# Attention scores contracted over 64 partitions a head, with unpadded keys, in a fused attention and MLP kernel on one Trainium2 core

The kernel runs on one core of one Trainium2 chip. The metric is the device time of one execution, in microseconds (us). The kernel before takes 275.12 us (median of 2 runs, 274.87 to 275.37).

## The reference

Causal attention over 4 batches, 8 heads, 768 positions and head size 64, then an MLP. Heads 0, 2 and 6 ("retrieval") see all earlier positions; the other five ("streaming") see 4 sink positions and a window of 64.

```python
scores = scale * np.matmul(q, k.transpose(0, 1, 3, 2))      # q, k: (4, 8, 768, 64), scaled by 0.1
mask   = np.where(retr, causal, causal & (is_sink | in_win))
a      = softmax(np.where(mask, scores, -1e9))
x      = np.matmul(a, v).transpose(0, 2, 1, 3).reshape(3072, 512)
h      = x @ w_in                                           # (512, 2048)
out    = np.maximum(0.01 * h, h) @ w_out                    # (2048, 512)
```

## The kernel before

The kernel works on 8 chunks of 384 positions (two a batch). The engines run in a fixed order; the attention of chunk n+1 is woven between the MLP matmuls of chunks n and n-1.

For each pair of heads, TensorE transposes keys and queries (both heads at once: 2 x 64 = 128 partitions). The queries are copied out in one piece. The keys are copied in two, each head into a tile of its own whose other 64 partitions are zero:

```python
kt = [bf(f"kt{i}", 4, 2, S) for i in range(2)]         # pair, half, position
def zeros(i):
    nc.vector.memset(kt[i][64:128, :, 0, :], 0.0)
    nc.vector.memset(kt[i][0:64, :, 1, :], 0.0)
    ...
# prep_pair
for hh in range(2):
    r = slice(64 * hh, 64 * hh + 64)
    move(eng[hh], kt[i][r, p, hh, CH * c : CH * c + CH], pt[r, 0, 0:3, :])
move(eng[2], qts[n][:, p, :], pt[:, 1, 0:3, :])
```

A score matmul then contracts over all 128 partitions, and the zeros remove the other head's queries. The work is cut into *units*: one group of keys of a retrieval head (one or two matmuls), or a whole streaming head (six matmuls of 64 columns). The `qk` part of a unit (scores, exp, mask) is issued, and two slots later its `do_av` part.

```python
nc.tensor.matmul(s[:, off : off + w], lhsT=kt[i][:, p, hh, 128 * kj : 128 * kj + 128],
                 rhs=qts[n][:, p, lo:CH], ...)
```

The softmax here doesn't subtract the row's maximum and nothing guards it: scores larger than these inputs give would overflow.

Of the kernel before, what the change touches and what calls it, by code (L numbers as in the profile page):

```python
# [17 lines left out]
CH = 384  # L18
# [3 lines left out]
def kernel(  # L22
# [12 lines left out]
    nc = tc.nc  # L35
    B, H, S, D = q.shape
    assert (B, H, S, D) == (4, 8, 768, 64)
    NS = int(n_sink)
# [17 lines left out]
    def bank(tag, shape, dtype):  # L56
        return ps.tile(shape, dtype, name=tag, tag=tag, bufs=BANKS[tag])
# [44 lines left out]
    def bf(name, *shape):  # L102
        return one.tile([128, *shape], BF16, name=name)
# [5 lines left out]
    e_sink = bf("e_sink", 128)  # L109
    m_sink = bf("m_sink", H, D + 1)  # L110
    shift = bf("shift", 2, 128)
    kt = [bf(f"kt{i}", 4, 2, S) for i in range(2)]
    va = [bf(f"va{i}", 6, H, D + 1) for i in range(2)]
    vb = [bf(f"vb{i}", 5, H, D + 1) for i in range(2)]
    vs = [bf(f"vs{i}", H, D + 1) for i in range(2)]
    ksink = [bf(f"ksink{i}", 4, 128) for i in range(2)]
# [6 lines left out]
                                channel_multiplier=cm, pattern=pattern)  # L123

    def zeros(i):
        eng = nc.vector
        eng.memset(kt[i][64:128, :, 0, :], 0.0)
        eng.memset(kt[i][0:64, :, 1, :], 0.0)
        nc.gpsimd.memset(va[i][:, :, :, D], 1.0)
        nc.gpsimd.memset(ksink[i][:], 0.0)  # L130
        nc.gpsimd.memset(vs[i][:, 0, :], 0.0)

    def constants():
        make_identity(nc, ident)
        zeros(0)
        nc.gpsimd.memset(m_caus[:], 1.0)
        keep(m_caus[:], [[1, 128]], ALU.is_ge, 0, -1)
        nc.gpsimd.memset(m_win[:], 1.0)
        keep(m_win[:], [[0, 6], [-1, 64]], ALU.is_gt, 0, 1)
        keep(m_win[:], [[0, 6], [1, 64]], ALU.is_ge, 64, -1)  # L140

        nc.gpsimd.memset(shift[:], 0.0)
        nc.gpsimd.memset(e_sink[:], 0.0)
# [23 lines left out]
    qts = {}  # L167

    def qk_src(nm, n):
        pat = "p (g h d) -> p g h d" if n >= WIDE else "p (h g d) -> p g h d"  # L170
        return stage[nm, n].rearrange(pat, h=H, g=3)

    def v_src(n):
        return stage["v", n].rearrange("p (g h d) -> p g h d", g=3, h=H)
# [42 lines left out]
    def prep_pair(n, p, tag="pt", eng=("v", "v", "v")):  # L217
        b, c = divmod(n, 2)
        i = b % 2
        if p == 0:  # L220
            qts[n] = rot.tile([128, 4, CH], BF16, name="qt", tag="qt", bufs=2)
        pt = bank(tag, [128, 2, 4, 128], BF16)
        for e, nm in enumerate("kq"):
            for g in range(3):
                nc.tensor.transpose(pt[:, e, g, :], cast[nm, n][:, g, 2 * p : 2 * p + 2, :], ident[:])  # L225

        def move(e, dst, src):
            if n < WIDE:

                src = src.rearrange("p g t -> p t g")  # L230
                dst = dst.rearrange("p (t g) -> p t g", g=3)
            else:
                dst = dst.rearrange("p (g t) -> p g t", g=3)
            if e == "v":
                nc.vector.tensor_copy(dst, src)  # L235
            else:
                nc.scalar.activation(out=dst, in_=src, func=ACTF.Copy)

        for hh in range(2):
            r = slice(64 * hh, 64 * hh + 64)  # L240
            move(eng[hh], kt[i][r, p, hh, CH * c : CH * c + CH], pt[r, 0, 0:3, :])
        move(eng[2], qts[n][:, p, :], pt[:, 1, 0:3, :])


# [3 lines left out]
    class Attention:  # L248
# [32 lines left out]
        def sink(self, values=True):  # L281
            i, c = self.i, self.c
            if c == 0:
                for h in range(H):
                    if not IS_RETR[h]:
                        p, hh = h // 2, h % 2
                        r = slice(64 * hh, 64 * hh + 64)
                        nc.vector.tensor_copy(ksink[i][r, p, NS * h : NS * h + NS], kt[i][r, p, hh, 0:NS])
                if values:
                    self.sink_values()  # L290
            s = self.score()
            w = CH - self.sink_lo
            for p in range(4):
                nc.tensor.matmul(s[:, 0:w], lhsT=ksink[i][:, p, :], rhs=qts[self.n][:, p, self.sink_lo : CH],
                                 start=(p == 0), stop=(p == 3))
            self.at_sink = rot.tile([128, CH], BF16, name="at_sink", tag="at_sink", bufs=2)
            nc.scalar.activation(out=self.at_sink[:, self.sink_lo : CH], in_=s[:, 0:w], func=ACTF.Exp, scale=SM)

        def retr(self, h):
            p, hh = divmod(h, 2)  # L300
            i, c, n = self.i, self.c, self.n
            groups = [[(0, 0)], [(1, 128), (2, 256)]] if c == 0 else \
                [[(kj, 0)] for kj in range(4)] + [[(4, 128), (5, 256)]]
            r = []
            for grp in groups:
                box = {}

                def qk(grp=grp, box=box):
                    s = self.score()
                    a = rot.tile([128, CH], BF16, name="at", tag="at", bufs=6)  # L310
                    off = 0
                    for j, (kj, lo) in enumerate(grp):
                        w = CH - lo
                        nc.tensor.matmul(  # L314
                            s[:, off : off + w], lhsT=kt[i][:, p, hh, 128 * kj : 128 * kj + 128],
                            rhs=qts[n][:, p, lo:CH], start=(j == 0), stop=(j == len(grp) - 1),
                            skip_group_check=True)
                        off += w
                    nc.scalar.activation(out=a[:, 0:off], in_=s[:, 0:off], func=ACTF.Exp, scale=SM)  # L319
                    off = 0  # L320
                    for (kj, lo) in grp:
                        if kj >= 3 * c:
                            nc.vector.tensor_mul(a[:, off : off + 128], a[:, off : off + 128], m_caus[:])  # L323
                        off += CH - lo
                    box[0] = a

                def do_av(grp=grp, box=box):
                    off = 0
                    for (kj, lo) in grp:
                        for qi in range(lo // 128, 3):  # L330
                            o = off + 128 * qi - lo
                            self.av(p, hh, qi, box[0][:, o : o + 128], va[i][:, kj, h, :])
                        off += CH - lo

                r.append((qk, do_av, p))
            return r

        def stream(self, h):
            p, hh = divmod(h, 2)
            i, c, n = self.i, self.c, self.n  # L340
            box = {}

            def qk():
                s = self.score()
                a = ats[ats_i[0] % len(ats)]
                ats_i[0] += 1
                for m in range(6):
                    k0 = 64 * max(6 * c + m - 1, 0)
                    nc.tensor.matmul(  # L349
                        s[:, 64 * m : 64 * m + 64], lhsT=kt[i][:, p, hh, k0 : k0 + 128],  # L350
                        rhs=qts[n][:, p, 64 * m : 64 * m + 64], start=(m == 0), stop=(m == 5),
                        skip_group_check=True)
                av_ = a[:, :, 0:4:3, :]
                nc.scalar.activation(  # L354
                    out=av_, in_=s[:, 0:CH].rearrange("p (j e f) -> p j e f", j=3, e=2),
                    func=ACTF.Exp, scale=SM)
                m_ = (m_win0 if c == 0 else m_win).rearrange("p (j e) f -> p j e f", j=3)
                nc.vector.tensor_mul(av_, av_, m_)  # L358
                box[0] = a

            def do_av():
                a = box[0]
                for j in range(3):
                    t = 3 * c + j
                    ve = va[i][:, 0, h, :] if t == 0 else vb[i][:, t - 1, h, :]
                    self.av(p, hh, j, a[:, j, 0:2, :], ve)
                    self.av(p, hh, j, a[:, j, 2:4, :], va[i][:, t, h, :])

            return [(qk, do_av, p)]
# [107 lines left out]
    def preps(n):  # L477
        return [lambda p=p: prep_pair(n, p) for p in range(4)]
# [4 lines left out]
    lo, hi = slice(0, 4), slice(4, 8)  # L483
    k0, q0, v0 = qk_src("k", 0), qk_src("q", 0), v_src(0)
# [12 lines left out]
    nc.gpsimd.tensor_copy(ktb[:, :, hi], k0[:, :, hi])  # L497
    late_constants()
    prep_pair(0, 0, "pt", "vva")
    prep_pair(0, 1, "py", "aav")  # L500
    qk(*R0)
# [49 lines left out]
    a1 = Attention(1, po_tags=("po", "po", "po", "py")).slots(order=[0, 2, 6, 1, 3, 4, 5, 7])  # L551
    run(a1[0:6], merge(in_slots(0), a1[6:]))
    zeros(1)
    cast_qk(2)
    load(3, "k", eng=nc.gpsimd)
# [62 lines left out]
```

## Time and profile before

| | before |
|---|---|
| time, median | 275.12 us |
| span of the profile | 273.6 us |
| TensorE (PE) busy | 240.9 us, 88% |
| VectorE (DVE) / ScalarE (ACT) busy | 119.5 / 142.0 us |
| mean granted clock of TensorE | 0.994 |
| start of the MLP of chunk 2 / of chunk 7 | 94.8 / 239.1 us |

The last row cuts the run into three: a start in which PE waits now and then, a full stretch of 144.3 us in which it doesn't (attention of chunks 3 to 7 among the MLP matmuls), and the end, in which there is only the MLP. I call the middle one the full stretch; its ends are the first `w_in` matmuls of MLP chunks 2 and 7. The busy time of PE is a sum of durations that overlap, so the starts of matmuls are what to read.

In the lines of the profile, PSUM tiles have these names: `psS` scores, `po` attention times values, `pt` transposes, `ph` and `py` the two matmuls of the MLP (weights `w_in` and `w_out`). `kt` and `qt` are the transposed keys and queries, `at` and `ats` the exponentiated scores, `va` and `vb` the values and their copy shifted by 64 positions, `xs` the attention output.

### The profile page before, as it was taken

The page shows a single profiled execution, that of the slowest core. Times are in us where ns is not written, and L with a number is a line of the kernel's source. Part 1 is how long each engine was busy: PE and PEld are TensorE (multiplying, and loading weights), DVE is VectorE, ACT ScalarE, POOL GpSimd, SP SyncE. Part 2 cuts the span into 40 slices and gives each one's busy share as a digit, 9 for nine tenths or more (in the row PEclk, how much of TensorE's full clock was granted, in tenths as well). Part 3 has the DMA queues.
Part 4 walks back from the last instruction along what each step waited for, and adds up shares of the span by engine and source line. Part 5 has one row for each costly group of instructions (what it writes and reads, how often), then busy time and mean ns, then how long its engine had stood idle before and what let it go on. Part 6 is the DMA issues. An engine that isn't in the chain of part 4 may idle for free.

```text
span 273.6 us, 5398 instructions
## 1 busy us (share of the span) xinstructions
PE 240.9 (88%) x2164; PEld 148.4 (54%) x2164; DVE 119.5 (44%) x323; ACT 142.0 (52%) x309; POOL 70.8 (26%) x122
## 2 busy tenths in 40 slices
PE   1647498857897899999999999999999999999995
PEld 1426365635553456665666556665665566545544
DVE  5669315766633514544545335544463224311012
ACT  3545787726740076555464666555555676633300
POOL 5889279764520034000420043000000000000000
PEclk9999889999999999999999999999999999999999
DMA  7999999999931298109940795120111111001122
GB/s 214 269 214 185 249 218 206 231 226 200 212 86 40 80 226 156 39 2 185 201 118 4 151 198 136 38 78 2 41 40 56 45 38 41 4 37 38 38 79 77
DMA packets 58281, 32.11 MB, mean 117 GB/s; under 512 B 44816, under 2 KB 53264, under 8 KB 58256
## 3 DMA queue, kind: packets, MB, share of 16 engines
q1 hardware_dynamic: 51792, 21.12, 33.2%
q0 software_dynamic: 5664, 8.91, 17.3%
q10 hardware_dynamic: 800, 1.73, 2.9%
q8 instruction: 17, 0.28, 0.4%
q14 instruction: 8, 0.07, 0.1%
HBM read 27.26 MB, written 6.29 MB: 123 GB/s over the span
## 4 chain that ended last, share of the span: by engine, by line
PE 75%; DVE 13%; ACT 7%; issue 2%; DMA 2%; SPq 0%; ACTq 0%; DVEq 0%
PE py L444 27%; PE ph L431 25%; PE po L266 6%; PE psS L314 4%; PE pt L225 3%; PE psS L444 3%; DVE kt L235 3%; DVE ats L358 2%; DVE at L323 2%; DVE xs L378 2%; ACT at L319 2%; PE pt L384 2%; PE psS L349 2%; DMA f<-in_q_dram 2%; ACT ats L354 1%
## 5 line engine op out<-in xcount | busy, mean ns | idle before, releaser
L431 PE MATMUL ph<-xt,w_in_bf 128*128 128x384 bf16 x512 | 104.7, 327 | 0.0
L433 ACT ACTIVATE g<-ph 128x384 bf16<-128x384 f32 x128 | 62.9, 491 | 76.1 <-PE ph L431 75.1
L444 PE MATMUL py<-w_out_bf,g 128*128 128x512 bf16 (+1 forms) x352 | 91.2, 374 | 3.2 <-DVE o L449 2.9
L431 PEld LDWEIGHTS <-w_in_bf 128*128 128x128 bf16 x512 | 44.9, 98 | 24.7 <-issue 0.3
L444 PEld LDWEIGHTS <-g 128*128 128x128 bf16 x400 | 36.0, 97 | 31.2 <-issue 5.4
L319 ACT ACTIVATE at<-psS 128x384 bf16<-128x384 f32 x81 | 39.2, 489 | 13.2 <-PE psS L314 12.7
L323 DVE TENSOR_TENSOR at<-at,m_caus 128x128 bf16<-128x128 bf16 x72 | 20.1, 310 | 47.2 <-ACT at L319 46.9
L314 PE MATMUL psS<-qt,kt 128*128 128x384 bf16 (+2 forms) x104 | 27.3, 301 | 3.8 <-ACT at L319 3.8
L235 DVE COPY kt<-pt 64x384 bf16<-64x384 bf16 x54 | 20.3, 375 | 23.0 <-PE pt L225 22.5
L184 POOL CAST kb<-f 128x512 bf16<-128x512 f32 x21 | 12.7, 622 | 65.9 <-DMA f<-in_k_dram 65.7
L449 DVE COPY o<-py 128x512 f32<-128x512 f32 (+1 forms) x22 | 14.9, 678 | 32.6 <-PE py L444 32.6
L358 DVE TENSOR_TENSOR ats<-ats,m_win 128x384 bf16<-128x384 bf16 x40 | 15.7, 393 | 19.3 <-ACT ats L354 19.1
L266 PEld LDWEIGHTS <-at 128*128 128x128 bf16 x252 | 16.6, 102 | 10.9 <-issue 4.6
L266 PE MATMUL po<-va,at 128*128 128x65 bf16 x237 | 20.5, 199 | 0.0
L354 ACT ACTIVATE ats<-psS 128x384 bf16<-128x384 f32 x37 | 18.0, 488 | 4.7 <-PE psS L349 4.7
L378 DVE TENSOR_TENSOR xs<-po,linv 128x384 bf16<-128x384 f32 x31 | 17.3, 557 | 1.1
L225 PE MATMUL pt<-ident,kb 128*128 128x128 bf16 x81 | 9.1, 222 | 8.6 <-DVE kb L495 5.2
L385 ACT ACTIVATE xt<-pt 128x384 bf16<-128x384 bf16 x29 | 14.2, 488 | 3.3 <-PE pt L384 2.5
L225 PEld LDWEIGHTS <-kb 128*128 128x128 bf16 x96 | 7.9, 103 | 14.4 <-DVE kb L495 5.2
L349 PEld LDWEIGHTS <-kt 128*128 128x128 bf16 x240 | 12.7, 102 | 5.4
L184 POOL CAST qb<-f 128x512 bf16<-128x512 f32 x21 | 12.7, 615 | 10.1 <-DMA f<-in_q_dram 7.0
L189 POOL CAST va<-f 128x512 bf16<-128x512 f32 x21 | 13.0, 635 | 8.3 <-DMA f<-in_v_dram 8.2
(97 smaller groups left out, 227.8 us busy)
## 6 DMA issues: line engine op xcount, KB each, us to landing
out_dram<-o SPq DMA_DIRECT2D x23, 256.0 KB, 2.0
f<-in_v_dram SPq DMA_DIRECT2D x18, 256.0 KB, 5.0
f<-in_k_dram SPq DMA_DIRECT2D x12, 256.0 KB, 6.2
f<-in_q_dram SPq DMA_DIRECT2D x12, 256.0 KB, 5.4
w_in_bf<-in_moe_w_in_dram POOLq DMA_DIRECT2D x4, 512.0 KB, 10.0
w_out_bf<-in_moe_w_out_dram POOLq DMA_DIRECT2D x4, 512.0 KB, 13.1
f<-in_k_dram POOLq DMA_DIRECT2D x6, 256.0 KB, 12.2
f<-in_q_dram POOLq DMA_DIRECT2D x6, 256.0 KB, 13.3
```

The costliest lines, as they stand in the source:

```text
L184: nc.gpsimd.tensor_copy(tb[:, g], src[:, g])
L225: nc.tensor.transpose(pt[:, e, g, :], cast[nm, n][:, g, 2 * p : 2 * p + 2, :], ident[:])
L235: nc.vector.tensor_copy(dst, src)
L266: nc.tensor.matmul(o, lhsT=lhsT, rhs=rhs, start=first, stop=False, skip_group_check=True)
L314: nc.tensor.matmul(s[:, off : off + w], lhsT=kt[i][:, p, hh, 128 * kj : 128 * kj + 128], rhs=qts[n][:, p, lo:CH], start=(j == 0), stop=(j ...
L319: nc.scalar.activation(out=a[:, 0:off], in_=s[:, 0:off], func=ACTF.Exp, scale=SM)
L323: nc.vector.tensor_mul(a[:, off : off + 128], a[:, off : off + 128], m_caus[:])
L358: nc.vector.tensor_mul(av_, av_, m_)
L378: nc.vector.tensor_tensor(xs[:], po[:, :, :, 0:D], linv.to_broadcast([128, 3, 2, D]), op=ALU.mult)
L431: nc.tensor.matmul(ph[:, 0:CH], lhsT=w_in_bf[:, g, 128 * t : 128 * t + 128], rhs=xts[n][:, g, :], start=(g == 0), stop=(g == KG - 1))
L433: nc.scalar.activation(out=gs[n][:, t, :], in_=ph[:, 0:CH], func=ACTF.Prelu, alpha=0.01)
L444: nc.tensor.matmul(py[n][:, 0 : c1 - c0], lhsT=gs[n][:, ng, 128 * tt : 128 * tt + 128], rhs=w_out_bf[:, ng, c0:c1], start=(ng == 0), stop= ...
```

## The change

The intent: 64 partitions are all that a head needs. Without the zero halves, the keys of a pair are copied in one piece, and four memsets go.

```diff
-    kt = [bf(f"kt{i}", 4, 2, S) for i in range(2)]
+    kt = [bf(f"kt{i}", 4, S) for i in range(2)]
 ...
-        eng.memset(kt[i][64:128, :, 0, :], 0.0)
-        eng.memset(kt[i][0:64, :, 1, :], 0.0)
 ...
-        for hh in range(2):
-            r = slice(64 * hh, 64 * hh + 64)
-            move(eng[hh], kt[i][r, p, hh, CH * c : CH * c + CH], pt[r, 0, 0:3, :])
+        move(eng[0], kt[i][:, p, CH * c : CH * c + CH], pt[:, 0, 0:3, :])
 ...
+            rows = slice(64 * hh, 64 * hh + 64)
-                            s[:, off : off + w], lhsT=kt[i][:, p, hh, 128 * kj : 128 * kj + 128],
-                            rhs=qts[n][:, p, lo:CH], ...
+                            s[:, off : off + w], lhsT=kt[i][rows, p, 128 * kj : 128 * kj + 128],
+                            rhs=qts[n][rows, p, lo:CH], ...
```

(The streaming heads' matmuls change in the same way; the copy of the sink keys loses its index `hh`.)

## The prediction

> **What bounds the kernel now.** I read the page's row of busy tenths first, then busy time by stage in windows that I set at the stage borders, then the chain that ended last, and last the instructions one by one in a stage where TensorE never rests.
>
> ```profile
> PE   1647498857897899999999999999999999999995
> PEclk9999889999999999999999999999999999999999
> ```
>
> Each digit is a fortieth of the span, 6.84 us. TensorE has holes in the first fourteen slices (to about 94 us) and is full from there on, at full clock. The same in windows; the columns are busy time and instruction count of PE, PEld, DVE, ACT and POOL, then clock, DMA share, GB/s:
>
> ```profile
> 0.00:35.00 35.00, 17.32 (x192) 13.03 (x193) 21.64 (x55) 18.46 (x40) 25.18 (x51) 0.97 1.07 226
> ...
> 53.00:62.00 9.00, 5.68 (x50) 3.45 (x50) 6.46 (x14) 3.48 (x8) 5.11 (x8) 1.00 1.07 237
> ...
> 94.00:125.00 31.00, 31.00 (x298) 19.47 (x297) 13.12 (x38) 18.81 (x41) 5.64 (x9) 1.00 0.54 108
> ```
>
> So there are two regimes. From 94 to 243 us (chunks 3 to 7 of attention, woven into the two MLP matmuls of the chunks before) PE is busy 147.97 of 149 us, DVE and ACT only 40 to 60%: each nanosecond that TensorE loses or wins there moves the end, and DVE work is free. Before 94 us, PE waits in turn for evacuations, casts and loads: there the latency of single copies counts.
>
> Next, the instructions in the full regime (start, duration, line, count):
>
> ```profile
> 160.44 0.33 PE L314 MATMUL psS<-qt,kt 128*128 128x384 bf16 x1
> 160.60 0.19 PE L266 MATMUL po<-vb,ats 128*128 128x65 bf16 x1
> 160.63 0.20 PE L266 MATMUL po<-va,ats 128*128 128x65 bf16 x1
> ...
> 160.78 0.82 PE L431 MATMUL ph<-xt,w_in_bf 128*128 128x384 bf16 x4
> 161.43 0.38 PE L444 MATMUL py<-w_out_bf,g 128*128 128x512 bf16 x1
> ```
>
> Starts, not durations, give the cost. The 384-column score matmul is listed with 0.33 us but the next one starts 0.16 us later; a 65-column one is followed after 0.03 us; four 384-column ones take 0.65 us, 0.1625 us each. The listed duration is therefore about 0.165 us (0.327 mean less 0.1625) longer than the slot taken: a tail that consecutive matmuls overlap. All carry 128*128: the kernel never leaves the full array. Weight loads (PEld) run ahead and cost nothing visible.
>
> **What the Trainium skill says.** "TensorEngine Tiling (Array Packing)", section "Key Properties": "Changing tiling mode (not just tile) drains the TensorE". The kernel before never changes it, so its trace can't confirm or refute this; it is the point on which the case turns. "TensorE: Matmul & The Clock Gate", section "Single matmul latency", gives (398 + N)/2.4 ns for a warm, isolated matmul: 326 ns for N = 384, and the trace has 327. It counts 128 cycles of the latency as the passage through the array, 53 ns at 2.4 GHz. The same page's table "Why this matters for your kernels" says that a matmul with a small contraction takes as long as one with 128, and that the gain is in concurrent tiles. "Advanced Engine Details and Errata", section "The Read-Write Bubble", says that ScalarE and VectorE pay a memory latency for each instruction; the trace agrees in that copies of 64 and of 128 partitions cost the same:
>
> ```profile
> L235 DVE COPY kt<-pt 64x384 bf16<-64x384 bf16 x54 | 20.3, 375 | 23.0 <-PE pt L225 22.5
> L235 DVE COPY qt<-pt 128x384 bf16<-128x384 bf16 x24 | 8.6, 358 | 0.4
> L127 DVE MEMSET kt<- 64x1536 uint32 x2 | 2.7, 1338 | 1.6 <-PEq L599 1.2 <-issue 0.4
> L128 DVE MEMSET kt<- 64x1536 uint32 x2 | 2.7, 1338 | 0.7 <-issue 0.7
> ```
>
> **The change, part by part.**
>
> *Copies and memsets removed.* There are 32 pair preparations (8 chunks by 4 pairs). Each loses one of two key copies: about 28 on DVE at 375 ns (longer, 0.55 us, in the first two chunks) and 4 on ACT at 482 ns. Four memsets of 1.34 us go. DVE loses 28 x 0.38 + 5.35 = about 16 us of 119.5. From 94 us on this is worth nothing, as PE is full. What counts is what sits on the chain. Up to 35 us the chain contains seven second-half copies, at 7.50, 9.03, 12.40, 13.93, 26.03, 29.48 and 31.38 us: 4 on DVE of 0.57 and 3 on ACT of 0.49, 3.75 us. Then chunk 2:
>
> ```profile
> 53.17 1.34 DVE kt L127
> 54.51 0.36 issue
> 54.87 1.34 DVE kt L128
> 56.21 0.21 DVE kt L235
> 56.42 0.01 issue
> 56.43 0.36 DVE kt L235
> ```
>
> The transposes for this copy are done at 54.99 us (54.66 + 0.33), so without the memsets the copy starts near 55.03 instead of 56.21: 1.18 us. The second halves at 56.43, 58.15 and 59.88 are in the chain as well, 3 x 0.36 = 1.08 us. Sum 3.75 + 1.18 + 1.08 = 6.0 us at most. The two memsets at the start (1.19 to 4.22 us) hide behind the load of the first queries, which the chain follows until 5.45. Some of the 6.0 will meet the next wait (the first w_in weights, the GpSimd casts of chunk 2); I take 5.5 us.
>
> *Score matmuls.* Same count (108 of line 314, 240 of line 349), same columns, contraction 64: no faster each by the skill's table, and all matmuls of one unit (one key group of a retrieval head, or a streaming head) lie in the same half, so none run side by side inside a unit. No gain here.
>
> *Mode switches, new.* Each unit becomes an island of 64-row matmuls between 128-row ones (attention x V, transposes, MLP): one switch in, one out. An even chunk has 3 x 2 + 5 = 11 units, an odd one 3 x 5 + 5 = 20, so 124 units and 248 switches. In the full regime are chunks 3 to 7: 20 + 11 + 20 + 11 + 20 = 82 units, 164 switches, all exposed. Chunks 1 and 2 have 31 units, 62 switches, of which I count 0.6 as exposed, since PE is busy there but often waits; chunk 0 nothing. That makes 164 + 37 = 201 exposed switches. The price of one is an estimate with two ends: 53 ns, if only the passage through the array is lost (the skill's 128 cycles), and 165 ns, if the whole overlapped tail seen above is lost. 201 x 0.053 = 10.7 us; 201 x 0.165 = 33.2 us. I take 0.08 us, in the lower half[...]: 201 x 0.08 = 16.1 us.
>
> Sum: 275.1 - 5.5 + 16.1 = 285.7; with a fair chance that switches cost less, I say 285.
>
> **Rivals.**
>
> 1. *Switches cost nothing*, the copies alone count: 275.1 - 5.5 = 269.6, right at the border of 2%. For it: the copies and memsets stand in the chain plainly; the drain is stated by a page, not seen here. Against: that statement, and that a tuned kernel pays four memsets and 32 extra copies for full-array matmuls, which somebody presumably found worth it. I give it a fifth.
> 2. *The full tail is lost at each switch*: 275.1 - 5.5 + 33.2 = 302.8. For it: 0.165 us is what an isolated matmul takes beyond its slot.[...]
> 3. *Only the array's passage is lost*: 275.1 - 5.5 + 10.7 = 280.3, within 2%.
> 4. *The early gain is swallowed* by loads: the DMA share is over 1 until 62 us, and the weights and chunk 2 come through GpSimd's queue. Then 2 us of the 5.5 remain, and every case above is 3.5 us later. Against: chunk 1 was cast by 18 us and used at 24, so some slack exists.
>
> **Range and chances.** One in five near 269, a quarter at 274 to 282, the rest spread over 282 to 303: the range of 8 in 10 is 268 to 303. Faster by over 2% needs under 269.6, which even free switches only just reach: 0.13. Within 2% (269.6 to 280.6) needs switches under about 0.055 us: 0.22. Slower: 0.65.
>
> **What would show it.** The score matmuls should be listed as 64*128 with the same duration. In the full regime, the start of the matmul after a score unit should come 0.05 to 0.17 us later than the 0.16 us slot (a 65-column neighbour at 0.22 to 0.33 us after the 384-column one instead of 0.16), and the start of the unit should lie as much behind the matmul before. The stretch from the first to the last attention unit of chunks 3 to 7, 149 us now, should grow by 164 switches' worth, about 13 us. The early part should be about 5 us shorter up to 35 us and 62 us, less the switches of chunks 1 and 2, with one kt copy of 128x384 for each pair and no memset at 53 us. I am wrong if the stretch after 94 us keeps its length (no drain), if 64-row matmuls of different heads overlap so much that it shrinks, or if the first 62 us are as long as before (the gain was hidden).

## The result, and the profile after

The changed kernel takes 289.0 us (2 runs, 287.95 and 290.04). The ratio to the kernel before is 1.0496, 95% interval 1.0396 to 1.0595: slower. Ratios in this text are the mean time of one kernel's fast runs over that of the other's fast runs of the same rounds, so not quite the ratio of the medians quoted.

The page's rows of busy tenths and of granted clock, after:

```profile
PE   1488899889978999999999999999999999999995
PEclk9999699999999999999999999999999999999999
```

The holes before the 14th slice have become smaller, and yet the run is longer: TensorE is fuller with the same work. The clock row has a 6 in the fifth slice, where before it had an 8 in the fifth and one in the sixth: TensorE ran at half clock for 6.8 us in all, before for 3.4 us. How the run divides, in both kernels, in windows whose ends are the ends of the full stretch. First before, then after; columns as in the prediction:

```profile
94.80:239.10 144.30, 143.28 (x1331) 88.36 (x1329) 62.33 (x185) 85.96 (x187) 16.86 (x27) 1.00 0.40 87
```

```profile
92.70:253.80 161.10, 158.96 (x1307) 83.22 (x1329) 55.39 (x169) 86.03 (x187) 16.79 (x27) 1.00 0.35 78
```

The start is 2.1 us shorter (92.7 for 94.8), the full stretch 16.8 us longer (161.1 for 144.3), the end the same 34.5 us. Both stretches hold the same 1329 weight loads, run at full clock, and DVE works less in the second: nothing but TensorE itself got slower. (Some twenty matmul records are missing from the second trace: 1307 for 1331.) Single matmuls of the changed kernel in this stretch (start, duration, line, shape, count):

```profile
161.17 0.33 PE L310 MATMUL psS<-qt,kt 64*128 64x384 bf16 x1
161.44 0.27 PE L261 MATMUL po<-va,at 128*128 128x65 bf16 x3
161.54 0.81 PE L428 MATMUL ph<-xt,w_in_bf 128*128 128x384 bf16 x4
162.29 0.34 PE L310 MATMUL psS<-qt,kt 64*128 64x256 bf16 x2
```

The listed durations are close to those of before, but their ends are modelled. The starts are not the same. The score matmul of 161.17 is followed after 0.27 us, where before it was 0.16. The four `ph` matmuls from 161.54 fill 0.65 us, until 162.19, but the score matmul after them starts at 162.29. There is a hole of 0.1 us on each side of a unit. Taken over all matmuls after 94 us (medians of the distance from one start to the next, in ns):

| this matmul, next matmul | before | after |
|---|---|---|
| 512 columns at 128 rows, then 128 rows / 64 rows | 216 / - | 216 / 312 |
| 384 columns at 128 rows, then 128 / 64 | 162 / - | 162 / 258 |
| 384-column score, then a 128-row matmul | 162 | 265 |
| 64-column score, then a 128-row matmul | 29 | 122 |
| 64-column score, then another of its unit | 29 | 29 |

So 96 ns on the way in and 93 to 103 on the way out. The first step inside the new mode is longer too: from the first to the second 64-column score 39 ns instead of 29, and from the first to the second 65-column matmul after a unit 39 instead of 29. A unit of one matmul pays 96 + 103 + 10 = 209 ns; 16.8 us over 82 units is 205. The view of waits shows the same from the weight loads' side: where they waited for no other engine ("issue"), with the sum in us, the number and the longest. Before and after:

```profile
PEld L314 <- issue: 1.6, 4, 1.1
```

```profile
PEld L310 <- issue: 22.3, 59, 0.6
...
PEld L346 <- issue: 11.1, 31, 0.4
```

These sums hold the time of the preceding matmuls too, beside which the loads no longer run; they are not the loss, but a sign. Before, a weight load started together with the matmul in front of it, as here (a `PEld` line in the timeline is a weight load):

```profile
160.44 0.33 PE L314 MATMUL psS<-qt,kt 128*128 128x384 bf16 x1
160.44 0.38 PEld L266 LDWEIGHTS <-ats 128*128 128x128 bf16 x6
```

After, at 161.17 and 161.44, the load comes with its own matmul, 4 ns ahead of it:

```profile
161.17 0.09 PEld L310 LDWEIGHTS <-kt 64*128 64x128 bf16 x1 [0.42 <-issue]
161.44 0.15 PEld L261 LDWEIGHTS <-at 128*128 128x128 bf16 x3 [0.17 <-issue]
```

In the start, the part of the chain at the keys of chunk 2, where two memsets stood before:

```profile
55.41 0.44 PE pt L222 x6
55.85 0.02 issue
55.88 0.36 DVE kt L232
56.23 0.28 DVE qt L232
```

No memset, and one key copy for each pair. The group's line confirms that a copy of 128 partitions costs what one of 64 did:

```profile
L232 DVE COPY kt<-pt 128x384 bf16<-128x384 bf16 x27 | 10.2, 379 | 26.6 <-PE pt L222 26.2
```

### The profile page after: what moved, and what is told of

Read it like the earlier page. It is cut to its first block, busy times and chain, and to the rows that moved or that the text cites.

```text
span 288.3 us, 5322 instructions
## 1 busy us (share of the span) xinstructions
PE 265.5 (92%) x2135; PEld 143.8 (50%) x2164; DVE 100.0 (35%) x291; ACT 140.4 (49%) x305; POOL 70.6 (24%) x122
## 4 chain that ended last, share of the span: by engine, by line
PE 84%; DVE 7%; ACT 5%; issue 2%; DMA 1%; SPq 0%; ACTq 0%
PE ph L428 27%; PE py L441 25%; PE po L261 10%; PE psS L310 7%; PE pt L222 4%; PE psS L441 3%; PE psS L346 3%; PE pt L381 2%; DMA f<-in_q_dram 1%; DVE ksink L283 1%; DVE ats L355 1%; ACT ats L351 1%; DVE o L446 1%; PE psS L289 1%; ACT g L430 1%
## 5 line engine op out<-in xcount | busy, mean ns | idle before, releaser
L428 PE MATMUL ph<-xt,w_in_bf 128*128 128x384 bf16 x512 | 105.9, 330 | 0.1
L441 PE MATMUL py<-w_out_bf,g 128*128 128x512 bf16 (+1 forms) x324 | 85.7, 374 | 3.9 <-DVE o L446 2.4
L319 DVE TENSOR_TENSOR at<-at,m_caus 128x128 bf16<-128x128 bf16 x72 | 17.3, 269 | 63.1 <-ACT at L315 62.7
L310 PE MATMUL psS<-qt,kt 64*128 64x384 bf16 (+2 forms) x104 | 28.2, 309 | 1.6 <-ACT at L315 1.6
L261 PE MATMUL po<-va,at 128*128 128x65 bf16 x237 | 21.2, 203 | 0.0
L310 PEld LDWEIGHTS <-kt 64*128 64x128 bf16 x108 | 8.4, 95 | 24.6 <-issue 22.3
L261 PEld LDWEIGHTS <-at 128*128 128x128 bf16 x252 | 13.7, 102 | 12.4 <-issue 9.1
L232 DVE COPY kt<-pt 128x384 bf16<-128x384 bf16 x27 | 10.2, 379 | 26.6 <-PE pt L222 26.2
L375 DVE TENSOR_TENSOR xs<-po,linv 128x384 bf16<-128x384 f32 x31 | 17.3, 557 | 1.1
L186 POOL CAST va<-f 128x512 bf16<-128x512 f32 x21 | 13.1, 636 | 9.6 <-DMA f<-in_v_dram 9.5
L346 PEld LDWEIGHTS <-kt 64*128 64x128 bf16 x240 | 9.5, 98 | 11.7 <-issue 11.1
```

Of the source, the lines that this page charges most:

```text
L261: nc.tensor.matmul(o, lhsT=lhsT, rhs=rhs, start=first, stop=False, skip_group_check=True)
L310: nc.tensor.matmul(s[:, off : off + w], lhsT=kt[i][rows, p, 128 * kj : 128 * kj + 128], rhs=qts[n][rows, p, lo:CH], start=(j == 0), stop=( ...
L346: nc.tensor.matmul(s[:, 64 * m : 64 * m + 64], lhsT=kt[i][rows, p, k0 : k0 + 128], rhs=qts[n][rows, p, 64 * m : 64 * m + 64], start=(m == ...
L428: nc.tensor.matmul(ph[:, 0:CH], lhsT=w_in_bf[:, g, 128 * t : 128 * t + 128], rhs=xts[n][:, g, :], start=(g == 0), stop=(g == KG - 1))
L441: nc.tensor.matmul(py[n][:, 0 : c1 - c0], lhsT=gs[n][:, ng, 128 * tt : 128 * tt + 128], rhs=w_out_bf[:, ng, c0:c1], start=(ng == 0), stop= ...
```

## The experiments

All twelve runs. The theory: each change between 64-row and 128-row matmuls costs 0.1 us of TensorE's time, nothing else got slower, and the copies' gain is real but partly taken up by other waits. The rivals: the cost belongs to each 64-row matmul or weight load; it belongs to the new layout; it comes with any contraction under 128; the copies gain nothing. The record calls a run slow when it is over 1.5% above the fastest of its kernel. All profiled runs were fast. Ratios are of fast runs alone, while the medians are of all runs, slow ones included (two of four in e8, one of four in e6, two of 22 in e11). Runs are told with their time, and with two marks read from the one profile of each: the length of the start, and that of the full stretch.

| run | median us | ratio, 95% interval | start | full stretch |
|---|---|---|---|---|
| before | 275.12 | | 94.8 | 144.3 |
| the changed kernel | 289.0 | 1.050 (1.040 to 1.060) | 92.7 | 161.1 |
| e1_mode_only | 298.29 | 1.082 (1.077 to 1.088) | 101.4 | 161.2 |
| e2_retr_only | 292.98 | 1.065 (1.062 to 1.069) | 100.2 | 156.5 |
| e3_stream_only | 280.70 | 1.020 (1.017 to 1.024) | 95.7 | 149.4 |
| e5_retr_96 | 275.67 | 1.001 (0.999 to 1.003) | 95.6 | 144.4 |
| e4_copies_only | 272.37 | 0.988 (0.983 to 0.993) | 93.4 | 144.2 |
| e8_copies_vfirst | 269.29 | 0.967 (0.964 to 0.971) | 86.0 | 144.2 |
| e6_pairs | 292.29 | 1.056 (1.051 to 1.062) | 95.1 | 160.2 |
| e6b_pairs_128 | 291.19 | 1.057 (1.053 to 1.060) | 99.7 | 154.3 |
| e7_hoist | 274.66 | 0.997 (0.995 to 0.998) | 93.6 | 144.3 |
| e9_hoist_vfirst | 276.41 | 1.005 (1.000 to 1.009) | 96.3 | 144.2 |
| e10_hybrid | 275.40 | 1.002 (0.998 to 1.006) | 95.5 | 144.2 |
| e11_hybrid_plain | 274.00 | 0.995 (0.993 to 0.997) | 93.2 | 144.2 |

In the runs the kernel before was at 275.31 to 275.61 us. The full stretch repeats to 0.2 us between profiles without switches; the start varies by some 2 us with when the clock is halved, and is read with that care. The profiles of e1 and e2 have 10.2 us at half clock in the start, that of before 3.4. A stretch of 3.4 us at half clock can cost up to 1.7 us, so these two starts may be up to 3.4 us too long for that reason alone.

### e1_mode_only: the matmuls changed, the copies not

```diff
 # the kernel before: padded keys, split copies, memsets
-    lhsT=kt[i][:, p, hh, 128 * kj : 128 * kj + 128], rhs=qts[n][:, p, lo:CH]
+    lhsT=kt[i][rows, p, hh, 128 * kj : 128 * kj + 128], rhs=qts[n][rows, p, lo:CH]
 # and the same in stream()
```

> The kernel before with its padded keys, its split copies and its memsets, but score matmuls over 64 rows. Switch theory (each change between 64-row and 128-row matmuls costs about 0.1 us where TensorE is full): 82 units x 0.2055 us = 16.9 us after 94 us, plus some 3.7 us in chunks 1 and 2, so about 295 us, slower than the changed kernel by the value of the copies. Layout theory (the loss comes from the shared, unpadded key tile or from the single copies): back near 275 us.

Measured 298.29 us. The full stretch is 161.2 us, equal to that of the changed kernel, with the same holes (312, 258 and 265 ns at the same places). The layout theory falls: the whole loss of the full stretch comes from the rows of the score matmuls. Without the copies' gain the start is longer than the changed kernel's by 8.7 us, of which up to 1.7 can be the clock (10.2 us at half clock against 6.8): some 7 to 8.7 us is what the copies save when switches are there too.

### e2_retr_only and e3_stream_only: which part carries the cost

The retrieval heads have few, long matmuls (108 in 84 units), the streaming heads many short ones (240 in 40 units). The edit is that of e1, in `retr()` alone or in `stream()` alone.

> As the run before it, but only the retrieval heads' scores over 64 rows: 84 of 124 units and 108 of 348 matmuls. Switch theory: 57 units x 0.2055 = 11.7 us after 94 us plus about 2.5 us earlier, so about 289 us. Per-matmul theory (each 64-row matmul or weight load costs something, 16.9 us / 222 = 0.076 us): 72 x 0.076 = 5.5 us plus about 1.2, so about 282 us.

> Only the streaming heads' scores over 64 rows: 40 of 124 units and 240 of 348 matmuls. Switch theory: 25 units x 0.2055 = 5.1 us after 94 us plus about 1.2 us earlier, so about 281.5 us. Per-matmul theory: 150 x 0.076 = 11.4 us plus about 2.5, so about 289 us.

Measured 292.98 and 280.70 us. In the full stretch e2 has 57 entries into 64-row matmuls and loses 156.49 - 144.28 = 12.2 us, 0.214 us for each; e3 has 25 and loses 149.37 - 144.28 = 5.1 us, 0.204 us for each. The two sum to 17.3, against 16.9 for both together. The per-matmul theory wanted the opposite order, 5.5 and 11.4 us, and falls. e2's total is 4 us above the switch theory's number; most of that lies in its start (5.4 us longer than before, where I expected 2.5). Whether that is a higher price in the start or the clock, of which up to 3.4 us could come, one profile can't tell. e3's start was 0.8 us longer, where 1.2 was expected; its interval straddles 2%, so its verdict by the record is unclear, though it is clear of no change.

### e5_retr_96: fewer rows, same mode?

```diff
 # the kernel before, retr() only; its heads all lie in the lower half, rows 64 to 95 of their keys are zeros
-    lhsT=kt[i][:, p, hh, 128 * kj : 128 * kj + 128], rhs=qts[n][:, p, lo:CH]
+    lhsT=kt[i][0:96, p, hh, 128 * kj : 128 * kj + 128], rhs=qts[n][0:96, p, lo:CH]
```

> The kernel before with the retrieval heads' scores over rows 0 to 95 (all of them lie in the lower half, rows 64 to 95 are zeros in the keys, so the result is right). If the price is that of a change of tiling mode and 96 rows stay in the 128-row mode: 275 us, no gap at the units. If the price comes with any change in the number of active rows: like the run with 64 rows for the same heads, about 289 us.

Measured 275.67 us, ratio 1.001. The timeline of this run in the full stretch:

```profile
162.22 0.81 PE L445 MATMUL py<-w_out_bf,g 128*128 128x512 bf16 x3
162.87 0.33 PE L315 MATMUL psS<-qt,kt 96*128 96x384 bf16 x1
163.03 0.33 PE L266 MATMUL po<-vs,at_sink 128*128 128x130 bf16 x3
```

The matmul has 96 rows, and there is no hole: 0.65 us for the three of 512 columns, then 0.16 us. So it isn't the change in the number of rows that costs. 64 rows cost and 96 don't. That fits the Trainium skill's page "TensorEngine Tiling (Array Packing)", section "Available Configurations", which lists tilings of 128, 64 and 32 rows and none of 96. No run here has 32 rows.

### e4_copies_only: the copies changed, the matmuls not

```diff
 # the changed kernel
-    lhsT=kt[i][rows, p, 128 * kj : 128 * kj + 128], rhs=qts[n][rows, p, lo:CH]
+    lhsT=kt[i][:, p, 128 * kj : 128 * kj + 128], rhs=qts[n][:, p, lo:CH]
```

> The changed kernel with its single copies and without memsets, but score matmuls over all 128 rows of the unpadded keys: the result is wrong on purpose (each score is the sum over both heads of a pair). Switch theory: no gaps at the units, the 16.9 us after 94 us vanish, and the early gain is seen alone: 275.1 less 5 to 6 us, about 269.5 us. If the copies bring nothing (the next wait takes their place): 275 us. If something other than the switches slows the full regime: clearly over 275 us.

Measured 272.37 us, ratio 0.988. The comparison with the reference passed all the same: with q and k scaled by 0.1 the scores are near 0.01 and the softmax nearly flat, so this comparison hardly sees the scores. The holes are gone and the full stretch is 144.2 us. On the median the gain is half of what I expected, but the four runs fall in two groups: 270.61 and 270.72, close to the expected 269.5, and 274.01 and 274.02. The profiled run is of the longer group, and what follows is shown for it alone. In its profile the MLP of chunk 1 starts at 49.3 us instead of 54.8, 5.5 us earlier (the prediction had put 3.75 of its 6.0 us before this point, the rest behind it); the MLP of chunk 2 starts only 1.4 us earlier. Between them, in the view of waits and in the timeline:

```profile
PE po L261 <- DMA vb<-va: 6.6, 1, 6.6
```

```profile
57.93 0.23 PE L261 MATMUL po<-va,ats 128*128 128x65 bf16 x2
64.71 0.23 PE L261 MATMUL po<-vb,ats 128*128 128x65 bf16 x1 [6.55 <-DMA vb<-va]
```

TensorE arrives earlier at a streaming head of chunk 2, and the shifted copy of its values (`vb`, made by a DMA after GpSimd has cast the values) has not landed. This is the prediction's rival 4, through a load that it did not name. From 62.8 us on, still in that wait, the clock is granted at half for 6.8 us, which adds to it.

### e8_copies_vfirst: that wait taken away

```diff
 # e4, on GpSimd's queue
     cast_qk(2)
+    cast_v(2)
+    v_shift(2, nc.sync)
     load(3, "k", eng=nc.gpsimd)
     load(3, "q", eng=nc.gpsimd)
-    cast_v(2)
     load(3, "v", eng=nc.gpsimd)
-    v_shift(2, nc.sync)
```

> The single-copy kernel with 128-row matmuls (scores wrong on purpose, as before) and, on GpSimd, the value casts of chunk 2 and their shift by DMA ahead of the loads of chunk 3. In the single-copy run without this, 5.5 us were gained by the start of the second MLP chunk and 4.1 of them lost again in a 6.6 us wait of TensorE for the shifted values. Swallowing theory: the wait goes and most of the gain stays, 269 to 270.5 us. Rival (another load or cast stands right behind): no change from 272.4 us.

Measured 269.29 us on the median of four (scores again wrong). These fall in two groups: 266.15 and 266.66, the fast runs, from which the ratio of 0.967 comes, and 271.93 and 272.46. No wait of TensorE for the DMA of `vb` is left in the profile, which is of the fast group, and its start is 86.0 us, 8.8 less than before, with as much half clock (3.4 us). What the longer runs lost is not known. So the copies and memsets are worth up to 9 us if nothing stands behind them, more than the 5 to 6.5 expected.

### e6_pairs and e6b_pairs_128: half the switches

```diff
 # e6 from the changed kernel, e6b from the kernel before: slots() issues the qk parts of units t and t+1
 # back to back, and the do_av parts of units t-2 and t-1 in the next slot
-            for t in range(len(units) + LAG + 2):
+            for t in range(0, len(units) + LAG + 2, 2):
```

> The changed kernel with the score matmuls of two consecutive units issued back to back, which halves the switches. Switch theory: 41 x 0.2055 = 8.4 us less after 94 us and about 1.5 us less before, and a little more where two units of opposite halves run side by side: about 279 us, if the schedule itself costs nothing (the next run tells that). Per-matmul theory: no change, 289 us.

> Control: the kernel before (padded keys, 128 rows) with the same grouping of two units. Without switches the grouping should change little: 275 us, within 1% either way, unless the two score banks now make TensorE wait.

Measured 292.29 and 291.19 us. The control missed: the grouping itself costs 16 us. In part TensorE now waits longer for VectorE: its transposes of the attention output wait 6.7 us for `xs` (1.6 before; for their weight loads the sums are 16.7 and 5.2, but those hold time beside running matmuls). In the full stretch, 10.0 us longer than before, 6.7 are added idle time of TensorE; the rest I did not trace. e6 taken alone would have looked like a refutation. Against its control, which has the same order, e6's full stretch is 6.0 us longer (160.2 and 154.3) instead of 16.8, and TensorE is idle in it for 6.6 us instead of 7.8, so it works some 7.1 us longer. It has 45 entries instead of 82, for which 45 x 0.205 = 9.2 us were due. The rest is in lines such as these of e6:

```profile
164.17 0.28 PE L310 MATMUL psS<-qt,kt 64*128 64x256 bf16 x1
164.17 0.29 PE L346 MATMUL psS<-qt,kt 64*128 64x64 bf16 x4
164.29 0.22 PE L310 MATMUL psS<-qt,kt 64*128 64x128 bf16 x1
164.30 0.22 PE L346 MATMUL psS<-qt,kt 64*128 64x64 bf16 x2
164.45 0.39 PE L447 MATMUL py<-w_out_bf,g 128*128 128x512 bf16 x1
```

A retrieval unit (lower half) and a streaming unit (upper half) run at the same time: both take 0.28 us from the first start to the next matmul, way out included, where one after the other they would need 0.165 + 0.175 us, and 0.1 for the way out. The trace of the full stretch has 15 places where a 64-row matmul starts within 30 ns of a longer one; at some 0.16 us each that is an estimate of 2.4 us, which brings 9.2 to 6.8, near the 6.0 to 7.1 measured. So neighbours within the mode are nearly free (a 384-column score was followed by another 64-row matmul after 0.173 us, against 0.163 at 128 rows), and opposite halves even overlap; but in this kernel the three retrieval heads, with 15 of an odd chunk's 20 units, all lie in the lower half.

### e7_hoist: memsets moved, nothing else

```diff
 # the kernel before
+    nc.vector.memset(kt[1][64:128, :, 0, :], 0.0)
     prep_pair(0, 0, "pt", "vva")
+    nc.vector.memset(kt[1][0:64, :, 1, :], 0.0)
 ...
-    zeros(1)
+    zeros1()        # zeros(1) without the two memsets of kt
```

> The kernel before with the two memsets of the second key tile moved from 53 us into idle time of VectorE near 5.7 and 8.1 us. They stood in the chain for 1.18 us; about 0.15 us may be lost at the first key copy. Expected about 274.1 us, 0.4% less. If another wait stands behind them at 53 us: no change.

Measured 274.66 us against 275.61, ratio 0.997 (0.995 to 0.998): 0.95 us less, where 1.03 (1.18 less 0.15) was expected.

### e9, e10 and e11: looking for a version that beats both

e9 is e7 with the reordering of e8.

> The kernel before with the hoisted memsets and the same reordering. Its TensorE never waited for the shifted values, so the reordering should bring nothing here: about 274.5 us, equal to the run with the hoisted memsets alone. If the reordering helps in itself: below 273.5 us.

Measured 276.41 us, ratio 1.005. The reordering helped only where `vb` was waited for. That it costs something here is not shown: in e9's profile the MLP of chunk 0 starts at 37.1 us, in e7's at 35.3, but the reordered casts begin only at 46.9 us. Of the 2.7 us by which its start is longer than e7's, 1.8 arose before them.

e10 uses the 64-row scores where TensorE has slack, in chunk 0 only:

```diff
 # e9, and:
+    kc = bf("kc", 4, CH)                                # unpadded keys of chunk 0, one copy a pair
+    rows = slice(64 * hh, 64 * hh + 64) if n == 0 else slice(0, 128)
+    def keys(k0):
+        return kc[rows, p, k0 : k0 + 128] if n == 0 else kt[i][:, p, hh, k0 : k0 + 128]
 ...
+    nc.vector.tensor_copy(kt[0][0:64, :, 0, 0:CH], kc[0:64])       # ahead of v_shift_pe()
+    nc.vector.tensor_copy(kt[0][64:128, :, 1, 0:CH], kc[64:128])
```

> Right result. Chunk 0 alone uses unpadded keys and 64-row scores (TensorE has slack there, so its 11 units should cost nothing), and two VectorE copies spread these keys into the padded tile for later; all other chunks use 128 rows; memsets hoisted and values first as above. Four second-half copies leave the start of the chain (0.57, 0.49, 0.57 and 0.49 us, 2.1 us), two copies of about 0.5 us are added, which may or may not lie in the chain: about 272.5 us, 1% less than before. Rival: any 64-row matmul costs wherever it stands, then 274.5 us or more.

Measured 275.40 us: 1 us less than e9, though their intervals overlap, and none less than before. In its chain the hoisted memset runs until 7.39 us and the first key copy starts at 7.42, where the changed kernel had it at 6.98: one part of the edit stood in the other's way.

e11 is e10 without the reordering and with the memsets of `kt[1]` elsewhere: one after the two spreading copies, one after the last `prep_pair(1, ...)`.

> The hybrid again (64-row scores on unpadded keys in chunk 0 only), without the reordering of the values, and with the two memsets of the second key tile moved from near 6 and 8 us, where they delayed the first key copy of the hybrid to 7.42 us, to VectorE's idle time near 18 and 32 us. About 0.95 us from the memsets (as measured alone) and 1 to 2 us from the start: 272.5 to 273.5 us. Rival (the start's gain is given back before 94 us, as in the other hybrid): 274.7 us, as with the memsets alone.

Measured 274.00 us against 275.56 (22 and 27 runs), ratio 0.9945 (0.9925 to 0.9965). It gives a right result and beats both kernels, the one before by only 0.5%: less than expected. That TensorE has slack for the 11 units of chunk 0 is not borne out: see the starts of the MLPs in the next section. Its interval overlaps that of e7, so most of the gain may be the memsets alone.

## Why the prediction was right, point by point

The time fell into the range (268 to 303), 4 us above the 285 named, and slower was the likeliest. The parts:

- **Two regimes**: right. The full stretch grew by 16.8 us while the rest of the run became 2.1 us shorter, and 7 us less VectorE work in the full stretch won nothing there.
- **Score matmuls no faster each**: right; the same 0.33 us listed, the same 29 ns between neighbours of a unit, once past its first step (39 ns).
- **A change of mode has a price**: right, and the term of the sum that was mis-sized. I took 0.08 us for a switch; it measured 0.093 to 0.103, and 16.8 us / 82 = 0.205 us for a unit. The full stretch was due 164 x 0.08 = 13.1 us and lost 16.8. Neither end of my estimate holds: it is more than the passage through the array (53 ns) and less than the whole tail (165 ns). The upper end rested on listed durations, whose ends are modelled; that 327 ns agreed with the prediction's 326 measured nothing of a drain. The trace shows that the weight load for the new mode is not started beside the matmul of the old one, and begins some 92 ns after that matmul's slot has ended. How the 92 ns divide between the array running empty and anything else is open; no run separates them.
- **Switches in the start**: undersized, and put in the wrong place. I counted 37 exposed ones, 3.0 us, in chunks 1 and 2 and none in chunk 0. The MLPs of chunks 0, 1 and 2 start at 34.9, 54.8 and 94.8 us before and at 36.1, 61.1 and 101.4 in e1: 1.2, 6.3 and 6.6 later. From e4 (30.6, 49.3) to the changed kernel (32.6, 55.7) it is 2.0 and 6.3. So chunk 0 was not free, the attention of chunk 1, between the first two of these marks, paid most, and that of chunk 2 hardly anything. Some of it is the clock: e1 has two stretches of half clock more than before, the changed kernel up to there one more than e4, up to 1.7 us each. That leaves 3.2 to 6.6 us by the first pair and 4.6 to 6.3 by the second.
- **The copies' gain**: by the MLP of chunk 1 it is 5.5 us with switches (e1 to the changed kernel, in which the clock can have a part) and 5.5 without (before to e4). The whole was undersized, 5.5 against up to 9 (e8), and how it is swallowed depends on what is beside it. Alone it was cut to 1.4 us in the profile of e4, by the wait for `vb`. In the changed kernel the switches delay TensorE past that wait (the second DMA of `vb` lands at 62.8 us, its first matmul comes at 65.5), so the copies offset them. Gains and losses in the start do not add up singly: -1.4 (copies) and +6.6 (switches) give +5.2, while both together gave -2.1. The prediction also read the equal cost of copies of 64 and 128 partitions as agreement with the read-write bubble. It shows only that the number of partitions doesn't set the cost; a fixed part of each instruction was not separated.
- **The sum**: on the marks, -8.7 + 6.6 + 16.8 = 14.7 us, and the spans differ by 288.3 - 273.6 = 14.7. These parts add up by construction, since both in the start are differences from e1, so this is a ledger and not a check. That the start came out near (2.1 us shorter for 2.5) is luck: two errors, opposite in sign, nearly cancelled. The 4 us by which the total was missed are almost all the price of a switch in the full stretch.
- **What would show it**: the hole after a 384-column score was put at 0.22 to 0.33 us between starts and is 0.265; the stretch was to grow by about 13 us and grew by 16.8; the start was to be shorter by the copies less the switches, some 2.5 us, and is by 2.1. But up to 35 us it was to be some 5 us shorter and was only 2.3 (MLP of chunk 0 at 32.6 for 34.9), and at the MLP of chunk 1 it was 0.9 us behind (55.7 for 54.8): the switches of chunks 0 and 1 again.

## What to carry to other kernels

Padding a contraction of 64 to 128 with zeros cost TensorE no time here (29 ns between 64-column matmuls either way), while every small group of 64-row matmuls between 128-row ones cost 0.2 us; count the groups, not the matmuls. 64-row tiles may pay if many stand together and lie in both halves, so that they run side by side; e6 shows such pairs overlapping, but no run here has a kernel that gains from it. Price a saving off the main engine against the next load as well: the same copies were worth 1.2% with one DMA behind them and 3.3% without that wait.

## What the Trainium skill lacked or had wrong

- "TensorEngine Tiling (Array Packing)", section "Key Properties", says that a change of mode drains TensorE, and gives no price. These runs show 96 ns on the way from 128 to 64 rows and 93 to 103 ns on the way back at full clock, and 10 ns more on the first step after each. 96 active rows showed no such price: 162 and 216 ns before the unit, as without, and 167 instead of 163 ns after a 384-column score.
- "TensorE: Matmul & The Clock Gate", section "The mechanism", says in one place that weight loads overlap matmuls in flight only when the row group differs (in another it also allows the background weight buffer). In the trace before, loads of 128 rows start together with the matmul in front of them, which uses the same rows (both at 160.44 us), so the first statement is too narrow. What stopped the overlap here was the change of mode.
- No page says where the time of a switch goes. The prediction's lower end of 53 ns, an estimate from the 128 cycles in the section "Single matmul latency" of "TensorE: Matmul & The Clock Gate" (given there for the cold clock), would have been too low by 40 to 50 ns.
